# Moving four small VectorE sums from block 9 to block 1 of each chunk of a fused attention and MLP kernel

## The chip, the cores and the metric

The kernel runs on one core of one Trainium2 chip. The metric is the device time of one execution in microseconds, as a median of several executions. Every kernel was timed beside the kernel before, in the same rounds on the same chip; two experiments of different rounds are best compared through their ratios to it. The span of a profiled execution, from its first to its last instruction, is about 1.8 us shorter than its time.

Four engines matter here. TensorE does matmuls, VectorE elementwise work and reductions, ScalarE activations and copies, GpSimd elementwise work that the others have no time for. In the profile they are PE (its weight loads PEld), DVE, ACT and POOL.

## The reference

```python
# efficient attention, B, H, S, D = 8, 8, 576, 64
q_s = softmax(q, axis=-1)          # over the head dimension
k_s = softmax(k, axis=2)           # over the sequence
kv  = einsum('bhsd,bhse->bhde', k_s, v)
x   = einsum('bhsd,bhde->bhse', q_s, kv)   # -> (4608 tokens, 512)
# MLP with SiLU
h   = x @ w_in                     # w_in 512 x 2048
g   = h * sigmoid(h)
out = g @ w_out                    # w_out 2048 x 512
```

## The kernel before

The 4608 tokens are done in nine chunks of 512, `t` = 0 to 8. TensorE's program is a list of units ("blocks" below). In the steady state, the list for chunk `t` interleaves the first product of chunk `t` with the second product of chunk `t - 1`:

```python
ps_ = [lambda t=t, fb=fb: mm1(t, fb) for fb in (0, 8, 1, 9, 2, 10, 3, 11)]   # "p": plain blocks
gs = [lambda t=t, i=i: group(t, i) for i in (1, 2, 6, 5, 7, 4, 3)]           # "g": Strassen group
# "b": second product of t - 1, seven Strassen products (1, 2, 6, 5, 7, 4, 3) in two halves
...
plan(begin[t] + 2, lambda t=t: s_op(t - 1, 1))     # S1 for the second product
plan(begin[t] + 4, lambda t=t: s_op(t - 1, 2))     # S2
plan(begin[t] + 11, lambda t=t: s_op(t - 1, 3))    # S3
plan(begin[t] + 16, lambda t=t: s_op(t - 1, 4))    # S4
mix = "pbpbpbpbpbpbpbp", "ggbgbgbgbbgbgb"
...
x = begin[t] + 9 if t < NCH - 1 else begin[t]
plan(x, lambda t=t: (xs_op(t, 1), xs_op(t, 2), xs_op(t, 3), xs_op(t, 4)))
```

`plan(u, f)` emits `f` just before unit `u`, so it fixes where an instruction stands in its engine's queue. In the timelines below, VectorE and GpSimd work their queues in this order. The Strassen scheme takes seven block products of sums and differences of quarter matrices where eight products of the quarters would be needed; XS (of x), WS (of w_in), S (of g) and T (of w_out) are these sums and differences, formed by VectorE. A chunk is thus fifteen blocks of the *plain stage* and then fourteen of the *group stage*. Chunk 8 has the two stages the other way round.

Each plain block `mm1` fills one of the PSUM banks 0 to 3 in turn (PSUM is the memory that the products are written to). ScalarE then takes a tanh, and VectorE forms the SiLU product from it; only then is the bank free. The first group product needs banks 0 and 1, so it waits for the SiLU products of the last plain blocks in them:

```python
def mm1(t, fb):
    bank = hb[0] % hb[1]          # hb = [next bank, number of banks]
    hb[0] += 1
    mm1_mm(t, fb, bank, range(NC))
    mm1_silu(t, fb, bank)         # ScalarE tanh, then VectorE GT <- (sg + 1) * PS

def xs_op(t, i):                  # XS: four differences of quarters of x, 128 x 512 fp16 each
    in0, in1 = {...}[i]
    nc.vector.tensor_tensor(out=XS4[i - 1], in0=in0, in1=in1, op=ALU.subtract)
```

The attention for the next batch runs in between, in chunks 2 to 6: row sums of exp(q) on VectorE, the normalisation with them on GpSimd, and a cast of v on GpSimd:

```python
for i, x in enumerate((4, 6)):
    pl(x, lambda i=i, b=b: exp_q(b, i))                                       # ScalarE
    pl(x + 1, lambda i=i, b=b: (qsum(b, i), qnorm(b, i, nc.gpsimd)))          # VectorE, GpSimd
...
for i, x in enumerate((9, 12)):
    pl(x, lambda i=i, b=b: (exp_k(b, i), vcast(b, i, nc.gpsimd)))             # ScalarE, GpSimd
    ...
```

The softmax here doesn't subtract the row's maximum and nothing guards it: scores larger than these inputs give would overflow.

## Time and profile before

| | before |
|---|---|
| time, median of 4 | 318.47 us (318.40 to 318.48) |
| span of the profiled run | 316.8 us |
| TensorE busy, mean granted clock | 86%, 0.951 |
| VectorE, ScalarE, GpSimd busy | 67%, 58%, 21% |
| wait of TensorE's first group for VectorE's SiLU product | 32.0 us in 6 waits |

No engine is busy throughout, so the place to look is where TensorE stands still. From the waits view (engine, line, what it waited for, total us, times, longest us):

```profile
PE PS L357 <- DVE GT L247: 32.0, 6, 7.2
```

Line 357 is the group's matmul, line 247 the SiLU product. Five of the six waits are in chunks 2 to 6; the sixth, in chunk 7, is only 1.4 us. Here is TensorE's timeline around the wait in chunk 4 (start us, duration us, engine, line, operation; in brackets the idle time before it and what ended it):

```profile
150.27 1.03 PE L455 MATMUL PS<-T,S 128*128 128x256 f16 x8 [0.92 <-DVE ow L475]
151.14 1.03 PE L274 MATMUL PS<-XT,W 128*128 128x512 f16 x4
158.03 3.57 PE L357 MATMUL PS<-XT,W 128*128 128x256 f16 x16 [5.86 <-DVE GT L247]
```

The last plain block ends at 152.17 and the group starts at 158.03. Note also the 3.57 us of the group's first 16 matmuls: in chunk 7 the same 16 take 1.91 (granted clock 0.50 over those 3.57 us, 1.00 over the 1.91). In the same stretch VectorE is never idle:

```profile
147.94 1.34 DVE L144 TENSOR_REDUCE zq<-eq 128x18 f32<-128x1152 bf16 x1
...
149.52 0.69 DVE L475 SCALAR_TENSOR_TENSOR ow<-PS,sa 128x512 f32<-128x512 f32 x1
150.13 0.68 DVE L247 SCALAR_TENSOR_TENSOR GT<-sg,PS 128x512 f16<-128x512 f32 x1
150.73 1.40 DVE L320 TENSOR_TENSOR XS<-XT 128x512 f16<-128x512 f16 x1
152.16 1.26 DVE L320 TENSOR_TENSOR XS<-XT,XS 128x512 f16<-128x512 f16 x1
153.34 1.37 DVE L320 TENSOR_TENSOR XS<-XT 128x512 f16<-128x512 f16 x1
154.63 0.41 DVE L320 TENSOR_TENSOR XS<-XT,XS 128x512 f16<-128x512 f16 x1
154.97 0.68 DVE L247 SCALAR_TENSOR_TENSOR GT<-sg,PS 128x512 f16<-128x512 f32 x1
155.56 1.21 DVE L429 TENSOR_TENSOR GT<-GT 128x2048 f16<-128x2048 f16 x1
156.70 1.27 DVE L247 SCALAR_TENSOR_TENSOR GT<-sg,PS 128x512 f16<-128x512 f32 x2
```

This is the queue that the group waits for: a row sum (L144), a store sum (L475, a part of the second product added up for its store), the four XS sums (L320), S3 (L429) and the last SiLU products. The four XS operations have one shape, yet three take 1.26 to 1.40 us and one 0.41. GpSimd's timeline shows what ran beside them (two normalisations, then two casts, up to 154.44):

```profile
147.62 4.23 POOL L153 TENSOR_TENSOR eq<-eq,rzq 128x1152 bf16<-128x1152 bf16 x2 [28.82 <-DVE rzq L148]
151.79 2.65 POOL L91 CAST vaug<-vt 128x1152 bf16<-128x1152 f32 x2
```

The first XS sum ends at 152.13, 0.3 us after the normalisations, and the third at 154.71, 0.3 us after the casts; the fourth runs when GpSimd is done. Last, the stages as windows, chunks 3 to 6, each from its first plain block to that of the next (columns: window, its length, busy us and instruction counts of PE, PEld, DVE, ACT, POOL, granted clock, DMA share, GB/s):

```profile
102.27:137.90 35.63, 28.76 (x290) 21.09 (x288) 23.56 (x31) 21.73 (x27) 6.82 (x4) 0.95 0.54 147
137.90:174.47 36.57, 29.70 (x290) 21.57 (x288) 23.57 (x31) 21.73 (x27) 6.82 (x4) 0.91 0.52 143
174.47:211.52 37.05, 30.18 (x291) 21.74 (x289) 23.56 (x31) 21.73 (x27) 6.82 (x4) 0.91 0.53 141
211.52:247.14 35.62, 28.72 (x290) 21.00 (x288) 23.56 (x31) 21.73 (x27) 6.82 (x4) 0.95 0.21 44
```

### The profile page before, as it was taken

Reading aid. Unit: us, or ns where it says so; the run is one execution under the profiler, and the core shown is the slowest. Engines: PE = TensorE matmul, PEld = TensorE weight load, DVE = VectorE, ACT = ScalarE, POOL = GpSimd, SP = SyncE. Lnnn points to the kernel's source line nnn. Section 1 sums busy time; section 2 is a strip of 40 time slices with the busy share of each in tenths; the row PEclk is TensorE's granted clock in tenths of the full one; section 3 lists DMA queues with packets and bytes.
Section 4 is the critical chain, followed back from the end, with each engine's and each line's share of the span. In section 5 each row is a group of like instructions: output and inputs, shape, how many; then the busy total and the mean of one; then the engine's idle time right before and its main releaser. Section 6 shows DMA issues by size and latency. Waiting matters only on the chain.

```text
span 316.8 us, 6096 instructions
## 1 busy us (share of the span) xinstructions
PE 271.6 (86%) x2539; PEld 190.5 (60%) x2540; DVE 211.2 (67%) x294; ACT 182.4 (58%) x232; POOL 67.5 (21%) x62
## 2 busy tenths in 40 slices
PE   8799999988299955998299974999379989999994
PEld 3477544555177634875177642876257758887683
DVE  3867879679915697457924697257954774676762
ACT  4759665767057861779147871578427644856310
POOL 0827908007100080003500071000700000000002
PEclk9999999999679997999879997899979999999999
DMA  7999995988902388055742479033300500330343
GB/s 278 270 257 305 315 342 152 311 306 236 258 31 64 81 247 265 2 129 163 201 167 44 92 233 271 20 69 65 74 0 11 125 0 2 68 68 0 69 99 101
DMA packets 35500, 45.88 MB, mean 145 GB/s; under 512 B 16208, under 2 KB 20048, under 8 KB 35472
## 3 DMA queue, kind: packets, MB, share of 16 engines
q1 hardware_dynamic: 29568, 33.69, 38.8%
q0 software_dynamic: 5584, 11.54, 13.9%
q8 instruction: 20, 0.33, 0.4%
q10 hardware_dynamic: 320, 0.26, 0.3%
q14 instruction: 8, 0.07, 0.1%
HBM read 36.70 MB, written 9.44 MB: 146 GB/s over the span
## 4 chain that ended last, share of the span: by engine, by line
PE 49%; DVE 30%; ACT 12%; issue 4%; DMA 3%; SPq 1%; POOL 1%; DVEq 0%; ACTq 0%
PE PS L455 17%; PE PS L357 14%; DVE GT L247 9%; PE PS L274 7%; DVE XS L320 7%; PE PS L393 4%; DVE zq L144 4%; PE PS L254 3%; DMA vt<-in_v_dram 3%; ACT sg L246 3%; ACT GT L342 2%; DVE ow L475 2%; ACT L342 2%; DVE GT L429 2%; PE PS L224 2%
## 5 line engine op out<-in xcount | busy, mean ns | idle before, releaser
L247 DVE SCALAR_TENSOR_TENSOR GT<-sg,PS 128x512 f16<-128x512 f32 (+2 forms) x88 | 58.8, 678 | 29.1 <-ACT sg L246 28.7
L274 PE MATMUL PS<-XT,W 128*128 128x512 f16 (+1 forms) x288 | 71.3, 373 | 1.1 <-DVE GT L247 0.8
L246 ACT ACTIVATE sg<-PS 128x512 f32<-128x512 f32 (+2 forms) x88 | 51.7, 597 | 34.0 <-PE PS L274 29.6
L153 POOL TENSOR_TENSOR eq<-eq,rzq 128x1152 bf16<-128x1152 bf16 x13 | 27.5, 2118 | 145.1 <-DVE rzq L148 145.1
L455 PEld LDWEIGHTS <-GT 128*128 128x128 f16 x512 | 49.6, 98 | 13.1 <-issue 1.2
L333 ACT COPY h<-PS 128x1024 f32<-128x1024 f32 x21 | 21.2, 1011 | 59.8 <-PE PS L357 59.8
L455 PE MATMUL PS<-W,GT 128*128 128x256 f16 x384 | 49.1, 273 | 0.0
L357 PE MATMUL PS<-XT,W 128*128 128x256 f16 x112 | 21.1, 369 | 32.0 <-DVE GT L247 32.0
L455 PEld LDWEIGHTS <-S 128*128 128x128 f16 x384 | 38.8, 101 | 14.4 <-issue 4.8
L336 DVE TENSOR_TENSOR h<-PS,h 128x1024 f32<-128x1024 f32 x21 | 25.7, 1225 | 30.9 <-PE PS L357 26.4
L357 PEld LDWEIGHTS <-W 128*128 128x128 f16 x168 | 20.0, 119 | 39.8 <-issue 33.7
L274 PEld LDWEIGHTS <-W 128*128 128x128 f16 x288 | 27.9, 98 | 22.3 <-issue 2.4
L455 PE MATMUL PS<-T,S 128*128 128x256 f16 x256 | 35.1, 285 | 3.7 <-DVE ow L475 3.7
L357 PEld LDWEIGHTS <-WS 128*128 128x128 f16 x224 | 21.5, 100 | 4.3 <-issue 1.2
L475 DVE SCALAR_TENSOR_TENSOR ow<-PS,sc 128x512 f32<-128x512 f32 x7 | 4.8, 692 | 28.5 <-ACT sc L471 28.5
L342 ACT ACTIVATE GT<-h 128x1024 f16<-128x1024 f32 x21 | 22.2, 1058 | 2.1 <-DVE h L336 2.1
L357 PE MATMUL PS<-XS,WS 128*128 128x256 f16 x168 | 22.5, 279 | 0.0
L89 ACT CAST XT<-PS 128x1024 f16<-128x1024 f32 (+2 forms) x18 | 17.4, 964 | 7.6 <-PE PS L224 7.6
L108 ACT ACTIVATE eq<-qt 128x1152 bf16<-128x1152 f32 x16 | 18.6, 1160 | 2.8 <-DMA qt<-in_q_dram 2.8
L676 POOL DMA_DIRECT2D out_dram<-ow x4 | 2.2, 552 | 82.3 <-DVE ow L661 82.3
L111 ACT ACTIVATE ek<-kt 128x1152 bf16<-128x1152 f32 x16 | 18.7, 1169 | 1.3 <-DMA kt<-in_k_dram 1.3
L144 DVE TENSOR_REDUCE zq<-eq 128x18 f32<-128x1152 bf16 x12 | 16.1, 1344 | 3.8 <-ACT eq L108 3.8
(76 smaller groups left out, 337.3 us busy)
## 6 DMA issues: line engine op xcount, KB each, us to landing
out_dram<-ow SPq DMA_DIRECT2D x64, 128.0 KB, 2.4
qt<-in_q_dram SPq DMA_DIRECT2D x12, 576.0 KB, 4.8
kt<-in_k_dram SPq DMA_DIRECT2D x12, 576.0 KB, 5.5
vt<-in_v_dram SPq DMA_DIRECT2D x12, 576.0 KB, 6.3
qt<-in_q_dram POOLq DMA_DIRECT2D x4, 576.0 KB, 12.9
kt<-in_k_dram POOLq DMA_DIRECT2D x4, 576.0 KB, 13.2
vt<-in_v_dram POOLq DMA_DIRECT2D x4, 576.0 KB, 12.5
W<-in_moe_w_out_dram POOLq DMA_DIRECT2D x4, 512.0 KB, 15.0
```

The source lines that it names most:

```text
L111: nc.scalar.activation(out=half(ek, cc), in_=jgd(b, "kt", cc), func=ACT.Exp)
L144: nc.vector.reduce_sum(out=z, in_=e, axis=AX.X)
L153: eng.tensor_tensor(out=e, in0=e, in1=r[:, :, :, None].to_broadcast([128, J, 2, D]), op=ALU.mult)
L246: nc.scalar.activation(out=s, in_=i, func=ACT.Tanh, scale=OS)
L247: nc.vector.scalar_tensor_tensor(out=o, in0=s, scalar=1.0, in1=i, op0=ALU.add, op1=ALU.mult)
L274: nc.tensor.matmul(out=PS[:, bank, o0:TCH], lhsT=W1[:, c, fb * 128:(fb + 1) * 128], rhs=XTS[t % 2][:, c, o0:TCH], start=(c == 0), stop=(c ...
L320: nc.vector.tensor_tensor(out=XS4[i - 1], in0=in0, in1=in1, op=ALU.subtract)
L333: nc.scalar.copy(out=H[i], in_=PS[:, 0:2, :].rearrange("p b n -> p (b n)"))
L336: nc.vector.tensor_tensor(out=H[i], in0=PS[:, 2:4, :].rearrange("p b n -> p (b n)"), in1=H[i], op=ALU.add)
L342: nc.scalar.activation(out=group_out(t, f, n), in_=x, func=ACT.Silu, scale=1.0 / XS)
L357: nc.tensor.matmul(out=PS[:, bank + p // 2, (p % 2) * HT:(p % 2 + 1) * HT], lhsT=a[:, c, p * 128:(p + 1) * 128], rhs=bb[:, c, :], start=(i ...
L455: nc.tensor.matmul(out=PS[:, bank, m * HN:(m + 1) * HN], lhsT=a[:, fc, m * 128:(m + 1) * 128], rhs=bb[:, fc, :], start=(first and fc == 0) ...
```

## The change

The intent is to take XS out of the queue ahead of the first group and to do it early in the chunk, where VectorE has gaps and GpSimd is idle. Two smaller moves come with it: the second row sum goes one block on, which puts it behind the store sum, and chunk 2 starts at PSUM bank 3 instead of 1.

```diff
-        x = begin[t] + 9 if t < NCH - 1 else begin[t]
+        x = begin[t] + (1 if t < NCH - 1 else 0)
         plan(x, lambda t=t: (xs_op(t, 1), xs_op(t, 2), xs_op(t, 3), xs_op(t, 4)))
...
-    plan(begin[2], lambda: (hb.__setitem__(0, 1), hb.__setitem__(1, 4)))
+    plan(begin[2], lambda: (hb.__setitem__(0, 3), hb.__setitem__(1, 4)))
+    plan(begin[3], lambda: hb.__setitem__(0, 1))
...
-                pl(x + 1, lambda i=i, b=b: (qsum(b, i), qnorm(b, i, nc.gpsimd)))
+                pl(x + 1 + i, lambda i=i, b=b: (qsum(b, i), qnorm(b, i, nc.gpsimd)))
```

Below, these are called the XS move, the bank order and the row-sum move.

## The prediction

> **What bounds it now.** In five of the repeated chunks (first products of 2 to 6) TensorE starves once. In the timeline of a typical one TensorE runs its fifteen plain blocks from 137.9 to 152.2, then idles 5.86 us until 158.03, released by VectorE's last SiLU product (the waits view: 32.0 us in all, 6 times). VectorE's backlog there: two 1.34 us row sums, a store sum, then the four XS sums, which take 1.40, 1.26, 1.37 and 0.41 us (4.2 us together), while GpSimd runs two normalisations and two casts (147.62 to 154.44). In the next-to-last chunk, where GpSimd is quiet, the same four take 0.42 us each (1.5 us), and TensorE waits 1.4 us there. Also, TensorE waits 0.92 us for the store sum that stands behind the second row sum; and the long idle makes the granted clock fall to 0.5, so the first group's 16 matmuls take 3.3 to 3.6 us instead of 1.9.
>
> [...]
>
> **What the change does.** It removes no work. XS goes to just after the first SiLU product, where VectorE has idle gaps of 1.0 and 1.55 us and GpSimd nothing to do: 4 x 0.34 = 1.4 us there, inside those gaps; S2 then ends about 145.0, still before its use at 145.7. The second row sum goes behind the store sum, so the 0.92 us wait goes. In the first chunk the banks start at a free one: 0.8 us of wait (at 64.95) goes.
>
> **New order, typical chunk**, estimated from these: second row sum ends 150.1, two SiLU products 151.3; S3[...] now meets the second normalisation and waits for its end, about 152.3, ends 153.4; two SiLU products end 154.6. The group starts about 154.7 instead of 158.0: 3.3 us gained in each of four chunks = 13. In the first, T3 and T4 also meet the casts: about 2 to 2.7.
>
> **Clock.** The idle shrinks from 5.9 to about 3.6 us. [...] The trace agrees on the period (drops at 80.90, 121.86, 155.99, 193.54 and 231.09, multiples of 3.413 apart), but a window some 20% busy still dropped it, one 42% busy did not. So 3.6 us is borderline. Slow clock costs these four chunks some 8 us now (from first group to next chunk 15.5 to 16.9, against about 14 with full clock); I expect 5 of them back.
>
> **Sum.** 318.45 - 13 - 2.5 - 5 = about 298 us. Range 292.5 to 304 (8 in 10). Chances: faster by over 2% 0.94, same 0.05, slower 0.01.
>
> **What would show it.** XS at 0.42 us each right after the chunk's first SiLU product; no 0.9 us wait before product 5; wait for the SiLU product before the first group 3.3 to 4 us in four chunks, about 6 in the first; S3 at about 2 us instead of 1.21; chunks of 31 to 32.5 us instead of 35.6 to 37.1.
>
> **What would make it wrong.** S3 losing to the casts as well (up to 2.5 us more per chunk, about 305 to 308); clock falling in every chunk (302 to 304) or in none (294); the early sums delaying S2 and product 6; a new limit on ScalarE.

## The result, and the profile after

The changed kernel took 300.24 us (median of 4, 299.6 to 302.32) against 318.47. The ratio is 0.9439, 95% interval 0.9391 to 0.9487. Here and below a ratio is the mean time of one kernel's runs over the mean of the other's runs of the same rounds, so it is not quite the ratio of the medians quoted. Executions over 1.5% slower than the fastest of the same kernel are left out of the means. The mean granted clock of the profiled run was 0.959, hardly above the 0.951 of before.

TensorE's wait in the waits view, and its timeline in chunk 4:

```profile
PE PS L357 <- DVE GT L247: 20.8, 7, 4.0
```

```profile
143.20 1.04 PE L455 MATMUL PS<-T,S 128*128 128x256 f16 x8
144.07 1.03 PE L274 MATMUL PS<-XT,W 128*128 128x512 f16 x4
148.79 3.26 PE L357 MATMUL PS<-XT,W 128*128 128x256 f16 x16 [3.69 <-DVE GT L247]
```

The 0.92 us stop is gone, the idle ahead of the group is 3.69 us, and the group's first 16 matmuls are still slow. VectorE in the same chunk:

```profile
134.68 0.42 DVE L320 TENSOR_TENSOR XS<-XT 128x512 f16<-128x512 f16 x1
135.14 0.42 DVE L320 TENSOR_TENSOR XS<-XT,XS 128x512 f16<-128x512 f16 x1
135.48 0.42 DVE L320 TENSOR_TENSOR XS<-XT 128x512 f16<-128x512 f16 x1
135.81 0.42 DVE L320 TENSOR_TENSOR XS<-XT,XS 128x512 f16<-128x512 f16 x1
...
142.56 1.34 DVE L144 TENSOR_REDUCE zq<-eq 128x18 f32<-128x1152 bf16 x1
...
145.25 2.29 DVE L429 TENSOR_TENSOR GT<-GT 128x2048 f16<-128x2048 f16 x1
147.46 1.27 DVE L247 SCALAR_TENSOR_TENSOR GT<-sg,PS 128x512 f16<-128x512 f32 x2
```

GpSimd's second normalisation, which ends at 146.46:

```profile
144.34 2.12 POOL L153 TENSOR_TENSOR eq<-eq,rzq 128x1152 bf16<-128x1152 bf16 x1 [0.59 <-ACT ek L111]
```

XS now costs 0.42 us each. S3 (L429) has taken its place beside this normalisation, and takes 2.29 us instead of 1.21. The chunks:

```profile
98.01:131.92 33.91, 30.13 (x291) 21.79 (x289) 22.64 (x31) 21.74 (x27) 7.43 (x4) 0.90 0.57 158
131.92:164.26 32.34, 28.56 (x291) 21.04 (x289) 22.62 (x31) 21.73 (x27) 7.43 (x4) 0.95 0.60 162
164.26:196.92 32.66, 28.88 (x290) 21.27 (x288) 22.63 (x31) 21.72 (x27) 7.43 (x4) 0.95 0.59 160
196.92:229.19 32.27, 28.47 (x290) 20.97 (x288) 22.63 (x31) 21.73 (x27) 7.43 (x4) 0.95 0.23 48
```

Split at the start of the first group, the four chunks read as follows. From the first plain block to the group: 20.12 or 20.13 us before, 16.87 or 16.88 after, so 3.25 us a chunk and 13.0 in all. From the group to the next chunk: 15.5, 16.4, 16.9 and 15.5 before, 17.0, 15.5, 15.8 and 15.4 after, so 0.7 us in all. By the start of chunk 3 the changed kernel leads by 102.27 - 98.01 = 4.3 us. These make 18.0 us, and the spans differ by 17.9.

### The profile page after: what moved, and what is told of

It reads as the page before. It is cut to its first block, busy times and chain, and to the rows that moved or that the text cites. A ratio compares the mean times of both kernels' runs of the same rounds, so it can differ in the third digit from the quotient of the medians.

```text
span 298.9 us, 6097 instructions
## 1 busy us (share of the span) xinstructions
PE 269.3 (90%) x2540; PEld 189.4 (63%) x2540; DVE 206.8 (69%) x294; ACT 182.4 (61%) x232; POOL 72.1 (24%) x62
## 4 chain that ended last, share of the span: by engine, by line
PE 56%; DVE 23%; ACT 11%; issue 4%; DMA 2%; POOL 1%; SPq 0%; DVEq 0%; ACTq 0%
PE PS L455 22%; PE PS L357 14%; PE PS L274 11%; DVE GT L247 7%; DVE zq L144 4%; DVE GT L429 4%; PE PS L393 3%; PE PS L254 3%; DMA vt<-in_v_dram 2%; DVE ow L475 2%; ACT L342 2%; PE PS L224 2%; ACT GT L342 2%; ACT sg L246 2%; ACT h L333 2%
## 5 line engine op out<-in xcount | busy, mean ns | idle before, releaser
L247 DVE SCALAR_TENSOR_TENSOR GT<-sg,PS 128x512 f16<-128x512 f32 (+2 forms) x88 | 58.1, 675 | 21.8 <-ACT sg L246 21.0
L274 PEld LDWEIGHTS <-W 128*128 128x128 f16 x288 | 27.9, 98 | 21.3 <-issue 1.3
L357 PE MATMUL PS<-XT,W 128*128 128x256 f16 x112 | 19.8, 347 | 20.8 <-DVE GT L247 20.8
L357 PEld LDWEIGHTS <-W 128*128 128x128 f16 x168 | 19.0, 113 | 28.0 <-issue 22.6
L91 POOL CAST vaug<-vt 128x1152 bf16<-128x1152 f32 x12 | 20.4, 1730 | 0.0
```

Of the source, the lines that this page charges most:

```text
L91: eng.tensor_copy(o, i)
L247: nc.vector.scalar_tensor_tensor(out=o, in0=s, scalar=1.0, in1=i, op0=ALU.add, op1=ALU.mult)
L274: nc.tensor.matmul(out=PS[:, bank, o0:TCH], lhsT=W1[:, c, fb * 128:(fb + 1) * 128], rhs=XTS[t % 2][:, c, o0:TCH], start=(c == 0), stop=(c ...
L357: nc.tensor.matmul(out=PS[:, bank + p // 2, (p % 2) * HT:(p % 2 + 1) * HT], lhsT=a[:, c, p * 128:(p + 1) * 128], rhs=bb[:, c, :], start=(i ...
```

## The experiments

Eleven kernels were run. All gave a correct result. All but one were timed in five rounds, e7 in three. Times are medians of all executions of a kernel.

| run | what | time, us | ratio to before (95%) |
|---|---|---|---|
| e1 | XS move alone | 292.27 | 0.9179 (0.9144 to 0.9214) |
| e2 | row-sum move and bank order, no XS move | 322.01 | 1.0091 (1.0067 to 1.0115) |
| e5 | XS and row-sum move | 303.84 | 0.9515 (0.9491 to 0.9538) |
| e6 | XS move and bank order | 292.33 | 0.9145 (0.911 to 0.9179) |
| | whole change | 300.24 | 0.9439 (0.9391 to 0.9487) |
| e3 | whole change, idle filled with matmuls | 294.75 | 0.9245 (0.9227 to 0.9263) |
| e4 | whole change, S3 late | 279.46 | 0.8762 (0.8745 to 0.8779) |
| e8 | e4 with other banks | 274.38 | 0.8596 (0.8579 to 0.8612) |
| e11 | e8, row sum moved back | 278.20 | 0.8743 (0.8719 to 0.8767) |
| e10 | e4 with XS back at block 9 | 311.61 | 0.9785 (0.9761 to 0.9809) |
| e7 | before, casts planned later | 319.29 | 1.0003 (0.998 to 1.0026) |
| e9 | before, casts held back | 307.44 | 0.966 (0.9633 to 0.9687) |

The first theory was: the gain is the shorter VectorE queue ahead of the first group, the clock that falls in the remaining idle holds most of the rest, and the two small moves are harmless. The rivals: the small moves carry part of the gain; or the group stage is held up by ScalarE or VectorE and not by the clock.

### e1: the XS move alone

```diff
-        x = begin[t] + 9 if t < NCH - 1 else begin[t]
+        x = begin[t] + (1 if t < NCH - 1 else 0)
```

> Only the four XS sums move (block 9 to block 1); second row sum and bank order as before. If the gain is the shortened VectorE queue ahead of the first group: XS at 0.42 us each, the first group starts 3.2 to 3.7 us earlier in each of four chunks, time 296 to 303 us. The 0.9 us wait of TensorE before product 5 should stay, splitting the idle in two, so the clock may fall less often than after the whole change. If the row sum's new place or the bank order carries a real part of the gain: 305 us or more.

It took 292.27 us (291.31 to 295.91), 3.7 us under the expected range and 8 us *less* than the whole change. TensorE in chunk 4 of this kernel, and the window of that chunk:

```profile
141.07 1.03 PE L455 MATMUL PS<-T,S 128*128 128x256 f16 x8 [0.92 <-DVE ow L475]
141.94 1.03 PE L274 MATMUL PS<-XT,W 128*128 128x512 f16 x4
144.97 1.91 PE L357 MATMUL PS<-XT,W 128*128 128x256 f16 x16 [2.01 <-DVE GT L247]
```

```profile
128.70:159.09 30.39, 27.38 (x291) 20.38 (x288) 22.03 (x31) 21.72 (x27) 7.42 (x4) 1.00 0.62 172
```

The 0.92 us stop stays, the idle ahead of the group is 2.01 us, the clock stays at 1.00, and the 16 matmuls take 1.91 us. The chunk is 30.39 us. S3 took 1.60 us here. Without the row-sum move the second normalisation starts 0.6 us earlier in the chunk, and S3 waits less for it: it ends 0.52 us after S3's start (142.65 and 142.13), against 1.21 us after the whole change (146.46 and 145.25). So the XS move is the gain, and some other part of the change takes 8 us of it away. My theory had not foreseen that, and was changed: the row-sum move joins two idles and makes S3 wait longer, and so loses time. Its rival is that the bank order does. e5 and e6 below were made to tell these apart.

### e2: everything but the XS move

```diff
-    plan(begin[2], lambda: (hb.__setitem__(0, 1), hb.__setitem__(1, 4)))
+    plan(begin[2], lambda: (hb.__setitem__(0, 3), hb.__setitem__(1, 4)))
+    plan(begin[3], lambda: hb.__setitem__(0, 1))
-                pl(x + 1, lambda i=i, b=b: (qsum(b, i), qnorm(b, i, nc.gpsimd)))
+                pl(x + 1 + i, lambda i=i, b=b: (qsum(b, i), qnorm(b, i, nc.gpsimd)))
```

> The second row sum one block on and the new bank order, XS left at block 9. Theory of the VectorE queue: the queue ahead of the first group holds the same work, and the second normalisation on GpSimd starts some 0.6 us later, so XS is blocked as long as before; the 0.9 us wait goes but is added to the long idle. 317 to 321 us (same). Rival, that these parts matter: under 312 us.

It took 322.01 us, 0.9% more than before, 1 us above the expected range. The expectation erred in that XS would be blocked only as long as before. The wait ahead of the group is 7.54 us in chunks 3 to 6, against 5.86: the removed 0.92 is in it, and 0.76 more, most of it in the first XS sum (2.08 us instead of 1.40), which meets the later normalisation. (Measured in e10 below, which has the same order there: that sum ends at 146.27, 0.3 us after the normalisation.)

### e3: the changed kernel with its idle filled

```diff
+    for t in range(2, NCH - 1):
+        plan(begin[t] + 15, lambda: heat(14, 7))    # 14 matmuls on constants, result unused
```

> The changed kernel with 14 matmuls on constant data into an unused bank put on TensorE just before the first group of chunks 2 to 6 (about 3.0 us of the idle, results unused). If the remaining cost is the clock that falls in the idle: the clock stays 1.0, the 16 matmuls of the first two groups take 1.9 us in every chunk, first group to next chunk about 14.0 us instead of 15.4 to 17.0, time 289 to 293 us, and the spread of runs (299.6 to 302.3) shrinks. If the group stage is held up by ScalarE or VectorE instead: 298 us or more.

It took 294.75 us (294.22 to 295.24), 1.75 us above the expected range. Part of that is a slip of mine: the edit also fills chunk 7, where the wait is only 1.4 us, and delays the group there by 1.45 us (243.78 - 229.19 from plain stage to group after the change, 237.40 - 221.36 here). The theory of the clock holds where it was tested: the mean granted clock is 0.997, the 16 matmuls take 1.91 us, and chunks 3 to 6 take 30.99 us each instead of 32.3 to 33.9, a group stage of 14.1 us. (The trace shows 13 of the 14 filling matmuls.)

```profile
141.63 2.97 PE L529 MATMUL PS<-warm 128*128 128x512 bf16 x13
145.27 1.91 PE L357 MATMUL PS<-XT,W 128*128 128x256 f16 x16 [0.67 <-DVE GT L247]
```

So the slow clock costs the changed kernel 7.2 us in chunks 3 to 6 (131.18 us for the four before the filling, 123.95 after). The chunk of e1, which also keeps its clock, is another 0.6 us shorter (30.39 against 30.99): that is S3 ending earlier. These are the two parts of what the change loses against e1 in those chunks: 7.2 us of clock and 2.4 of S3.

### e4: S3 behind the last SiLU product

```diff
-        plan(begin[t] + 11, lambda t=t: s_op(t - 1, 3))
-        plan(begin[t] + 16, lambda t=t: s_op(t - 1, 4))
+        plan(begin[t] + (15 if t < NCH - 1 else 11), lambda t=t: s_op(t - 1, 3))
+        plan(begin[t] + (17 if t < NCH - 1 else 16), lambda t=t: s_op(t - 1, 4))
-    plan(begin[2] + 12, lambda: t_op(3, nc.vector))          # T3, and the halves of T4, likewise
+    plan(begin[2] + 15, lambda: t_op(3, nc.vector))
...
```

> The changed kernel with S3 (and T3 in the first chunk) moved behind the last SiLU product, and S4 (and T4) behind the first group sum: they leave the VectorE queue that the first group waits for. If that queue still sets the start of the first group: it starts 2.2 us earlier in four chunks, TensorE's idle there falls to about 1.5 us, the clock stays up, time 280 to 286 us. If S3 was only waiting for something that will then hold the last SiLU products or the group sums instead: 292 us or more.

It took 279.46 us, half a microsecond better than expected. S3 is needed by product 7 in the group stage, not by the first group. Behind the last SiLU products it still meets GpSimd (its casts run from 135.39 to 138.64), and takes 2.18 us, but TensorE no longer waits for it:

```profile
133.10 2.41 DVE L247 SCALAR_TENSOR_TENSOR GT<-sg,PS 128x512 f16<-128x512 f32 x4
135.43 2.18 DVE L429 TENSOR_TENSOR GT<-GT 128x2048 f16<-128x2048 f16 x1
```

The wait ahead of the group is 1.48 us and the clock 0.999. The queue did still set the group's start.

### e5 and e6: which of the two small moves costs 8 us

e5 is the changed kernel with the bank order of before, e6 with the row sum of before:

```diff
-    plan(begin[2], lambda: (hb.__setitem__(0, 3), hb.__setitem__(1, 4)))     # e5
-    plan(begin[3], lambda: hb.__setitem__(0, 1))
+    plan(begin[2], lambda: (hb.__setitem__(0, 1), hb.__setitem__(1, 4)))
-                pl(x + 1 + i, lambda i=i, b=b: (qsum(b, i), qnorm(b, i, nc.gpsimd)))     # e6
+                pl(x + 1, lambda i=i, b=b: (qsum(b, i), qnorm(b, i, nc.gpsimd)))
```

> XS moved and the second row sum one block on; bank order as before. The XS move alone gave 292.3 us, the whole change 300.2: one of the two other parts costs 8 us. Theory: the row sum's new place does. It starts the second normalisation 0.6 us later, so S3 waits 2.29 instead of 1.60 us for GpSimd, and it removes the 0.92 us stop of TensorE before product 5, so the two idles of 0.92 and 2.01 us become one of about 3.7 us and the clock falls. Then 299 to 303 us here, with the clock under 0.97. Rival, the bank order: 291 to 294 us.

> XS moved and the new bank order; the row sum as before. Theory (the row sum costs the 8 us): 290 to 293 us, at most 1 us from XS alone, with the 2.01 us waits and a clock over 0.98. Rival, that the bank order costs them: 298 us or more.

e5 took 303.84 us, 0.8 us above the range of the theory, with a clock of 0.955 in the profile; e6 took 292.33 us. The row-sum move is the culprit. From the ratios it costs (0.9515 - 0.9179) x 318.5 = 10.7 us without the new bank order and (0.9439 - 0.9145) x 318.5 = 9.4 us with it, each uncertain by 1 to 2 us from the intervals. The bank order is worth 2.4 us beside the row-sum move (0.9515 - 0.9439), uncertain by 1.7, and next to the XS move alone e1 and e6 cannot be told apart.

The profile of e6 fell in a run classed as slow (294.44 us), and shows both outcomes of the same wait of 2.01 us. In two of four chunks the clock fell, from 1.00 to 0.50 at 115.31 and at 207.47, and the 16 matmuls took 2.67 and 3.33 us; in two they took 1.91:

```profile
114.33 2.67 PE L357 MATMUL PS<-XT,W 128*128 128x256 f16 x16 [2.01 <-DVE GT L247]
...
146.40 1.91 PE L357 MATMUL PS<-XT,W 128*128 128x256 f16 x16 [2.01 <-DVE GT L247]
...
176.79 1.91 PE L357 MATMUL PS<-XT,W 128*128 128x256 f16 x16 [2.01 <-DVE GT L247]
...
207.19 3.33 PE L357 MATMUL PS<-XT,W 128*128 128x256 f16 x16 [2.01 <-DVE GT L247]
```

The six runs of e1 go from 291.3 us at a clock of 0.994 to 295.9 (slow) at 0.983. Against that the clock fell at the wait of 3.69 us in all four such chunks of after (at 114.05, 148.18, 182.31 and 213.03). In e5, which has the same wait, the 16 matmuls took 3.57, 3.57 and 3.21 us in chunks 3 to 5.

### e7 and e9: is XS slow because of GpSimd?

e7 planned the two casts later in the kernel of before:

```diff
-                pl(x, lambda i=i, b=b: (exp_k(b, i), vcast(b, i, nc.gpsimd)))
+                pl(x, lambda i=i, b=b: exp_k(b, i))
+                plan(u + 16 + i, lambda i=i, b=b: vcast(b, i, nc.gpsimd))
```

> The kernel before, XS at block 9, with only GpSimd's two casts moved behind the second group product of the chunk. If XS was slow because each of its operations waited for one GpSimd instruction: the first still takes 1.4 us (it meets the second normalisation), the other three 0.42, the first group starts about 1.8 us earlier in five chunks, 306 to 311 us with the clock still falling. If XS is slow at block 9 for another reason: all times as before, 317 us or more.

It took 319.29 us, as before, and XS was as slow as before (1.40, 1.25, 1.37 and 0.41 us in chunk 4). That does not refute the theory, because the edit did not do what I meant. GpSimd has nothing else in its queue at that point, so the casts ran right behind the normalisations as they always had (in chunk 4 the two normalisations from 149.26 to 153.49, the two casts up to 156.08). The planned place only ordered the queue; it held nothing back. e9 puts a real dependence ahead of the casts:

```diff
-                pl(x, lambda i=i, b=b: (exp_k(b, i), vcast(b, i, nc.gpsimd)))
+                pl(x, lambda i=i, b=b: exp_k(b, i))
+            plan(u + 17, lambda: nc.gpsimd.tensor_copy(gate, H[0][0:1, 0:1]))   # waits for the group sum
+            for i in range(2):
+                plan(u + 17, lambda i=i, b=b: vcast(b, i, nc.gpsimd))
```

> The attempt to move the casts (e7) changed GpSimd's program order around nothing, so they ran when they had. Here one GpSimd copy of one element of the first group's sum stands before the casts and really holds them until that sum exists. Kernel before otherwise, XS at block 9. If each slow XS operation waits for one GpSimd instruction: the first XS operation still takes 1.4 us, the other three 0.42, the first group starts about 1.8 us earlier in five chunks, 305 to 311 us. If XS is slow at block 9 for another reason: all four times as before, 317 us or more.

It took 307.44 us. The edit has a side effect: the loads of k and v that followed in the loop now stand in the new loop, where `x` is always 12, so the first half of each is issued some blocks later. No wait shown here is for a load. XS in chunk 4, and the wait:

```profile
146.59 1.40 DVE L320 TENSOR_TENSOR XS<-XT 128x512 f16<-128x512 f16 x1
148.02 0.42 DVE L320 TENSOR_TENSOR XS<-XT,XS 128x512 f16<-128x512 f16 x1
148.36 0.42 DVE L320 TENSOR_TENSOR XS<-XT 128x512 f16<-128x512 f16 x1
148.70 0.42 DVE L320 TENSOR_TENSOR XS<-XT,XS 128x512 f16<-128x512 f16 x1
```

```profile
152.10 3.22 PE L357 MATMUL PS<-XT,W 128*128 128x256 f16 x16 [4.07 <-DVE GT L247]
```

Only the first XS sum, which meets the second normalisation, is still slow. The wait fell from 5.86 to 4.07 us. So, of the 4.2 us that XS took at block 9, 1.8 was waiting for the casts, about 1 waiting for the normalisation, and about 1.4 its own work.

### e10: S3 late, XS left at block 9

```diff
-        x = begin[t] + (1 if t < NCH - 1 else 0)       # against e4
+        x = begin[t] + 9 if t < NCH - 1 else begin[t]
```

> S3, S4, T3 and T4 behind the group's start as in e4, the row sum and bank order of the changed kernel, but XS left at block 9 as before. If only the measured length of the VectorE queue counts: against e2 (322 us, wait 7.5 us) S3 takes 1.1 us out of it per chunk, wait about 6.4 us, 313 to 318 us, the clock still falling in every chunk. If late S3 was the real lever and XS's place does not matter: under 300 us.

It took 311.61 us, 1.4 us under the range. The wait in chunks 3 to 6 is 6.40 us as expected, and the 16 matmuls behind it took 3.35, 3.57 and 3.46 us in chunks 3 to 5, not 1.91. What I had left out is chunk 2, where T3 and T4 left the queue as well: its first two group products end at 83.4 us, in e2 at 86.8. Leaving XS at block 9 costs 32 us against e4, so late S3 alone was not the lever. Both belong to one queue.

### e8 and e11: the last wait, and the row-sum move once more

e8 adds to e4 a bank order in which the last two plain blocks do not use the group's first banks. e11 then takes the row sum back.

```diff
-    plan(begin[3], lambda: hb.__setitem__(0, 1))                                      # e8, against e4
+    for t in range(3, NCH):
+        plan(begin[t], lambda: hb.__setitem__(0, 0))
-                pl(x + 1 + i, lambda i=i, b=b: (qsum(b, i), qnorm(b, i, nc.gpsimd)))   # e11, against e8
+                pl(x + 1, lambda i=i, b=b: (qsum(b, i), qnorm(b, i, nc.gpsimd)))
```

> Late S3 (279.5 us) with the plain blocks of chunks 3 and later starting at bank 0, so that the last two use banks 2 and 3 and the first group's banks 0 and 1 come free two blocks earlier. If the 1.4 to 1.5 us idle left before the first group is the wait for the last SiLU product of its own bank: the idle falls to about 0.4 us ahead of the first group (some of it returning ahead of the second), 273 to 277 us. If the SiLU queue as a whole sets it: 278 us or more.

> The fastest kernel (e8, 274.4 us) with the second row sum back in front of the store sum. In the change that move cost about 10 us, because it joined two idles. With the queue short there is no idle left to join, so the 0.92 us stop before product 5 comes back as plain loss, less 0.3 us that the second group waits anyway: 276 to 279 us. If moving the row sum back is good here as well: 273 us or less.

e8 took 274.38 us (273.81 to 274.87), 14% below before, and is the fastest kernel. Its chunks leave TensorE no idle to speak of:

```profile
119.62:147.12 27.50, 27.48 (x290) 20.25 (x288) 21.51 (x31) 21.72 (x27) 7.43 (x4) 1.00 0.71 192
```

e11 took 278.20 us. The same row-sum move that costs about 10 us in the change is worth 3.8 us here by the medians, 4.7 by the ratios (e8 and e11 were timed in different rounds): with no idle ahead of the group, the stop of 0.92 us before product 5 is plain loss.

## Why the prediction was right or wrong

The time, 300.24 us, lies inside the range of 292.5 to 304 and 2.2 us above the point of 298. Step by step:

- "XS at 0.42 us each right after the chunk's first SiLU product": right. Every XS operation of the trace took 0.42 us. That the slow ones had waited for GpSimd was tested by e9.
- "no 0.9 us wait before product 5": right in the trace. The text lists this beside the gains; its sum has no term for it, and there was no gain. The group stage started when VectorE's queue was done, whatever TensorE had done before. Ending the plain stage 0.92 us earlier only lengthened the idle, and the row sum's later place made S3 take 0.7 us longer (2.29 against 1.60 in e1). e5 and e6 put this part at 9 to 11 us lost, which the text did not see. This is the step that a prediction of the parts would have got wrong.
- "S3 at about 2 us instead of 1.21": 2.29. "3.3 us gained in each of four chunks = 13": 3.25 a chunk, 13.0.
- "wait for the SiLU product before the first group 3.3 to 4 us in four chunks": 3.69 in each. "About 6 in the first": 4.04 and 0.55 us, in two stops; 6.03 in e5, which lacks the new bank order.
- "2 to 2.7 us" in the first chunk: 4.3 by the start of chunk 3. About 0.4 us of it was gained before chunk 2, where the change touches nothing, and 0.8 is the removed wait at 64.95. From the second block of chunk 2 to chunk 3 it is 3.0 us (65.81 to 102.27 before, 64.57 to 98.01 after), and 2.1 in e5 (66.37 to 100.73). The new bank order lets half of the first group product run ahead of the last SiLU product there, which the estimate left out; that is the likely source of the other 0.9.
- "I expect 5 of them back" of the clock: 0.7 came back. This term was mis-sized. The text gives the reason for doubt, that a window 20% busy lowered the clock and one 42% busy did not, and then takes most of the gain nevertheless. The clock fell at the wait of 3.69 us in all four chunks; that 3.6 us would be borderline was an estimate. (A window is a stretch of 3.413 us here, counted from the clock's falls in the trace. By the trace of before, TensorE was busy for 0.65 us, 19%, of the one ahead of the fall at 80.90, and for 44% of the least busy one that kept the clock, 115.04 to 118.45.) e3 shows that the time was lost to the clock: with the idle filled, the mean granted clock is 0.997, the group stage takes 14.1 us, the "about 14" of the text, and 7.2 us come back in the four chunks.
- "chunks of 31 to 32.5 us": 32.3 to 33.9, two of the four inside, the clock again.

The two misses partly cancel (1.6 to 2.3 us more in the first chunk, 4.3 less from the clock), which is why the sum came out close. That the two offset each other is luck.

Two things that the sum rests on can be read from the traces. XS beside GpSimd: in e9 the first sum, which meets the second normalisation, took 1.40 us, the three with no GpSimd instruction beside them 0.42 each. The period of the clock: its falls in the trace of before (80.90, 121.86, 155.99, 193.54, 231.09) are 40.96, 34.13, 37.55 and 37.55 us apart, 12, 10, 11 and 11 times 3.413 us, and it stayed at 0.50 for 10.24, 3.41, 6.83, 6.83 and 3.41 us.

What stays open: whether e1 keeps its clock because its idle is split in two (0.92 and 2.01 us) or because it is shorter in all. No run separates these; in e6, which has the same two idles, the clock fell in two chunks of four. Nor does any run show whether GpSimd's or VectorE's instruction goes first if both are ready at the same moment.

## What to carry to other kernels

Find the instruction that releases the longest wait, list everything its engine does between the last gap and it, with measured durations, and ask of each entry whether the waiting engine needs it that early; here taking XS out was worth 26 us, and taking S3, T3 and T4 out another 21 on top of the whole change. Removing a stall upstream of a fixed release point gained nothing here (e2, ratio 1.0091), and joining two idles into one cost the clock as well (mean granted clock 0.994 in the profile of e1, 0.955 in that of e5): the same move of one row sum lost about 10 us with the queue long and won 4 with it short. A planned position ordered a queue but delayed nothing (e7, ratio 1.0003), so an experiment that means to delay work must give it a dependence.

## What the traces show of the clock, and of VectorE beside GpSimd

- In the traces of before and after the granted clock is 1.00 or 0.50, and every stretch at 0.50 that ends within the span lasts one, two or three times 3.413 us. With the spans divided into windows of that length from the first fall, and the matmuls' modelled times taken as busy, TensorE was at most 35% busy in the window that ended in a fall (after, 178.90 to 182.31), and at least 44% busy in every window that kept the full clock (before, 115.04 to 118.45). Not all the windows ahead of a fall were idle throughout: the clock fell after one with matmuls in its first 0.65 us of 3.41 (before, at 80.90), and in e6 (a run classed as slow) twice after 3.41 us with 1.4 us of matmuls around an idle of 2.01 us (111.90 to 115.31, 204.06 to 207.47). In the traces of before and after the clock came back after windows at least 78% busy at the halved clock (after, 213.03 to 216.45), and not after one 75% busy (after, 114.05 to 117.46). The idles of 3.69 us lowered the clock in all four chunks of after, at a cost of 7.2 us in 300.
- In the trace of before VectorE got its turn after each GpSimd instruction while both had work queued: three XS operations in a row took 1.40, 1.26 and 1.37 us, against 0.42 alone, and ended at 152.13, 153.42 and 154.71, each 0.3 us after one GpSimd instruction (151.85, 153.14 and 154.44).
- GpSimd took longer as well: its two casts took 2.25 us together with VectorE out of the way (e9), 2.65 between XS sums (before), 3.25 between S3 and S4 (after, 1.4 times) and 4.24 between S3, T3 and T4 (after, chunk 2, 1.9 times).
